# Sigmoid attention and a top-1 mixture of experts in one kernel: attention products in one group per seven steps

## The chip, the core and the metric

The kernel runs on one core of a Trainium2 chip. The metric is device time in microseconds (us) of one execution. Before the change the median of three runs is 801.93 us (801.66 to 802.69).

## What is computed

```
scores = q @ k^T / sqrt(64) - log(448)          # 8 batches x 12 heads, 448 x 64 each
x      = sigmoid(scores) @ v                    # tokens: 3584 rows of 768
logits = x @ w_gate                             # 8 experts
idx    = argmax(logits);  g = softmax(logits)[idx]
out    = g * (relu(x @ w1[idx]) @ w2[idx])      # 768 -> 1024 -> 768, the rows of each expert
```

All is float32 in and out.

## The kernel before

**Attention.** Two heads make a pair (48 pairs, index `g`), and two pairs make a unit (`u`, 24 of them). A unit has seven steps (`ST` = 7, index `s`); a step computes the scores of 64 keys of both pairs against all 448 queries (`scores(s)`, line 573), ScalarE turns them into sigmoids (`squash`, line 558), and `weighted(s)` (line 589) multiplies them with the values. All these products use quarters of TensorE's array (64 x 64), four at a time. Score tiles lie in a ring of four PSUM buffers (`sc`), and the small tiles of the gate lie in the same ring (`small_ps`). Three units make a batch of 448 tokens; a batch has 21 steps (`PB`).

**Loads.** `load_pair` brings k and q of a pair. The first two pairs come by rows and are turned by TensorE (`turn`, line 534), with a copy out of PSUM by VectorE for k and by ScalarE for q (line 537); the others come in blocks of 32 columns and are transposed by VectorE (line 542). `load_values` brings v. Loads are issued on the queues of SyncE (SP), of ScalarE (q of the first pairs) and of GpSimd (k and v of early pairs). `warm_up` issues products on a tile of ones at the start: 34 of them, and 12 more between the two pairs of step 0.

**Gate.** After a batch its logits (`gate_a`, `psg`), the choice (`gate_b`, `pl`), counts (`gate_c`, `pc`), ranks of the tokens within their expert (`gate_d`, `pr`), records scattered to memory (`gate_d2`, line 386, GpSimd indirect DMAs) and the gate's values as rows (`gate_g`, `gate_e`, `pg`, copied by ScalarE at line 415) follow, at steps that the tables `LATE`, `LAST`, `EARLY` and `FIRST_LATE` give: `7: "b"` is stage b at the batch's step 7. I call the products of `pl`, `pc`, `pr` and `pg` the rank products.

**Experts.** Each of seven slots runs all 448 tokens of a batch through one expert, the commonest of that batch (`moe`): 144 products of the first layer (line 213) and 144 of the second (line 236), each 128 x 128 by 448 columns, in parts of high and low bits. Weights are loaded raw, ScalarE casts the high part (line 132) and GpSimd subtracts to get the low part (line 133). What the slots don't cover is sorted into items afterwards, found by prefix sums on VectorE (`tensor_tensor_scan`, line 801), gathered, computed (`large`) and scattered.

**Order.** The whole order is written by hand: each engine gets its instructions in the order in which the program issues them. Up to step 70 (`START`) there is only attention and gate. From there the generator `attention()` yields twice per step and the caller issues 7 products of the experts at each yield (`more`). Attention products come in two groups per unit: at `i == 0` three pieces (24 score and value products of the built program), at `i == 3` five pieces (32). `until(n)` runs the experts' products up to n before the end of the slots.

Of the kernel before, what the change touches and what calls it, by code (L numbers as in the profile page):

```python
# [18 lines left out]
P = 128  # L19
# [5 lines left out]
def tile_sigmoid_attention_top1_moe(  # L25
# [457 lines left out]
    ops = {}  # L483
# [7 lines left out]
    def load_pair(g):  # L491
# [3 lines left out]
        if g < BY_ROWS:  # L495
            for nm, src, eng in (("k", k, nc.sync), ("q", q, nc.scalar)):
                t = apool.tile([P, KC, D], F32, tag=nm + "n", bufs=4, name=f"{nm}n_{g}")
                for h in range(2):
                    eng.dma_start(t[OWN[h]], src[b, 2 * hp + h].rearrange("(p c) d -> p c d", c=KC))
                ops[g, nm + "n"] = t  # L500
            return
# [12 lines left out]
    def load_values(g):  # L514
        if g >= NG or (g, "v") in ops:
            return
        b, hp = divmod(g, NP)
        t = apool.tile([P, KC, D], F32, tag="vn", bufs=4, name=f"vn_{g}")
        for h in range(2):
            eng = nc.gpsimd if 4 <= g < K_POOL else nc.sync  # L520
            eng.dma_start(t[quarter(g, h)], v[b, 2 * hp + h].rearrange("(p c) d -> p c d", c=KC))
        ops[g, "v"] = t

    def turn(g, nm):

        if g >= NG:
            return
        t = apool.tile([P, S], F32, tag=nm + "t", bufs=4, name=f"{nm}t_{g}")
        if g < BY_ROWS:
            rows = ops.pop((g, nm + "n"))  # L530
            ps = ps_moe.tile([P, 512], F32, tag="moe", name=f"turn_{nm}_{g}")
            for c in range(KC):
                for own in OWN:
                    nc.tensor.matmul(
                        ps[own, c * DK : (c + 1) * DK], rows[own, c, :], ident[own, own], start=True, stop=True
                    )
            (nc.vector.tensor_copy if nm == "k" else nc.scalar.copy)(
                t.rearrange("d (p c) -> d c p", c=KC), ps[:, :S].rearrange("d (c p) -> d c p", c=KC)
            )
            ops[g, nm] = t  # L540
            return
        nc.vector.transpose(t, ops.pop((g, nm + "n")).rearrange("p j s -> p (j s)"))
        ops[g, nm] = t

# [19 lines left out]
    def scores(s):  # L564
# [3 lines left out]
        for g, ps in zip(two, pss):  # L568
            if s == 0 and g == 1:
                warm_up(FILL)  # L570
            for h in range(2):
                ks = ops[g, "k"][OWN[h]].rearrange("d (p c) -> d c p", c=KC)[:, c]
                nc.tensor.matmul(ps[quarter(g, h), :S], ks, ops[g, "q"][OWN[h]], start=True, stop=True)  # L573
# [3 lines left out]
    def weighted(s):  # L577
# [22 lines left out]

    WARM, FILL, K_POOL, BY_ROWS = 34, 12, 22, 2
    START = 70
# [8 lines left out]
        1: lambda u: (turn(2 * u + 2, "q"), load_values(2 * u + 2)),  # L611
        3: lambda u: (turn(2 * u + 3, "k"), load_pair(2 * u + 5)),
        4: lambda u: (turn(2 * u + 3, "q"), load_values(2 * u + 3)),
    }

    def attention():
# [4 lines left out]
        warm_up(WARM)  # L621
        load_pair(0)
        load_pair(1)
        for g in range(2):
            turn(g, "k")
            turn(g, "q")
            load_values(g)
# [3 lines left out]
        for g in (2, 3):  # L631
            load_pair(g)
            load_values(g)
        done_av = done_sc = 0
# [35 lines left out]

        LATE = {7: "b", 10: "c", 11: ("l", "c2"), 12: "c3", 14: "d", 16: ("d2", "g"), 17: "e"}
        LAST = {3: "b", 5: "c", 6: ("l", "c2"), 7: "c3", 8: "d", 9: ("d2", "g"), 10: "e"}
        EARLY = {5: "b", 7: ("c", "c2"), 9: ("l", "c3"), 11: "d", 13: ("d2", "g"), 17: "e"}
        FIRST_LATE = {5: "b", 10: "c", 11: ("l", "c2"), 12: "c3", 14: "d", 16: ("d2", "g"), 17: "e"}
        PLACES = {}
# [15 lines left out]
        def stages_late(s):  # L691
            u, i = divmod(s, ST)
            b, r = divmod(s - PB, PB)
            if r == (3 if b < B - 1 else 1) and (b + 1) * PB >= START:
                gate_a(b)
# [3 lines left out]
        for s in range(N_ST + 11):  # L699
# [6 lines left out]
            if s < START:  # L706
                if s % 2 == 0:
# [4 lines left out]
                    score_to(s + 2)  # L712
            elif i == 0:
                stages_late(s)
                score_to(a + 2)
                weigh_to(a)
                score_to(a + 4)
            yield s, MIX[0]
            if s >= START:
                if i > 0:  # L720
                    stages_late(s)
                if i == 3:
                    weigh_to(a + 2)
                    score_to(a + 6)
                    weigh_to(a + 4)
                    score_to(a + 7)
                    weigh_to(a + 5)
            if i in READY and s < N_ST:
# [50 lines left out]
    def cut(n, w=1):  # L779
        return scr[:, n * NI : (n + w) * NI]  # L780
# [19 lines left out]
    for msk, cum in zip((big, few), rank):  # L800
        nc.vector.tensor_tensor_scan(cum, cut(3), msk, 0.0, op0=ALU.mult, op1=ALU.add)
    ends = rest.tile([P, 1], F32, name="ends")
    nc.vector.tensor_scalar(ends, rank[1][:, NI - 1 : NI], 1.0, None, op0=ALU.add)
# [299 lines left out]
```

## Time and profile before

| | |
|---|---|
| runs, median of 3 | 801.93 us |
| profiled execution, its own time | 803.83 us |
| profiled execution, span from first to last instruction | 801.9 us |
| PE (matmul) busy | 789.7 us, 98% |
| DVE, ACT, POOL busy | 355.1, 391.2, 360.3 us |
| DMA queue of SyncE, share of 16 engines | 63.1% |

PE is TensorE's matmul pipe, PEld its weight loads, DVE is VectorE, ACT ScalarE, POOL GpSimd, SP SyncE. A product's busy time runs over its successor's, since products are pipelined: what a product costs is the distance from its start to the next start. Float32 products of the attention stand as two records each in the trace, and as one row in the built order.

### The profile page before, as it was taken

To read this page: it belongs to the slowest core of one execution; us is meant where nothing else is said; L and a number is where in the kernel's file an instruction comes from. 1 tells how busy PE (TensorE), PEld (TensorE's weight loads), DVE (VectorE), ACT (ScalarE), POOL (GpSimd) and SP (SyncE) were. 2 spreads that over 40 slices of the span, in tenths; PEclk is the share of its full clock that TensorE was granted. 3 is DMA by queue.
4 is the path that set the end of the run, shared out by engine and by line. 5 is a ranking of instruction groups with operands and counts; after the bars stand their busy time and mean duration, and the time that the engine had idled before them with its cause. 6 is when DMAs were issued, how large, how long until landed. Compare 5 with 4: busy or idle time off the path is not lost. (4 is left out here: it accounts for less than half of the span.)

```text
span 801.9 us, 15879 instructions
## 1 busy us (share of the span) xinstructions
PE 789.7 (98%) x5726; PEld 613.6 (77%) x5726; DVE 355.1 (44%) x787; ACT 391.2 (49%) x711; POOL 360.3 (45%) x346
## 2 busy tenths in 40 slices
PE   9999999999999999999999999999999999999996
PEld 6655555777787778766777678777788998999996
DVE  2344456462535435362443525355267174334443
ACT  5877777454533554454544545355342342335342
POOL 8658665353223424243242334233553664574350
PEclk9999999999999999999999999999999999999998
DMA  9997998895669937489575874747166445556671
GB/s 178 157 180 129 169 218 183 181 214 110 145 136 200 197 74 166 114 189 183 106 168 99 195 173 113 182 123 182 50 162 169 138 134 158 162 135 176 190 216 38
DMA packets 312372, 124.09 MB, mean 155 GB/s; under 512 B 209502, under 2 KB 309934, under 8 KB 312288
## 3 DMA queue, kind: packets, MB, share of 16 engines
q1 hardware_dynamic: 305920, 110.80, 63.1%
q0 software_dynamic: 6048, 11.76, 6.1%
q8 instruction: 47, 0.77, 0.4%
q10 hardware_dynamic: 320, 0.46, 0.2%
q14 instruction: 37, 0.30, 0.1%
HBM read 100.89 MB, written 22.47 MB: 154 GB/s over the span
## 5 line engine op out<-in xcount | busy, mean ns | idle before, releaser
L558 ACT ACTIVATE at<-sc,bias_s 128x448 f32<-128x448 f32 x336 | 188.2, 640 | 114.2 <-PE sc L573 111.8
L133 POOL TENSOR_TENSOR w1l<-wst,w1h 128x768 fp32r<-128x768 f32 x72 | 132.3, 1846 | 206.5 <-ACT w1h L132 197.4
L133 POOL TENSOR_TENSOR w2l<-wst,w2h 128x512 fp32r<-128x512 f32 x84 | 107.0, 1294 | 155.5 <-ACT w2h L132 155.5
L573 PE MATMUL sc<-qt,kt 64*64 64x448 f32 x1344 | 171.2, 549 | 1.0 <-ACT at L558 0.7
L589 PE MATMUL av<-at,vn 64*64 64x448 f32 x1344 | 167.0, 539 | 0.8 <-ACT at L558 0.7
L573 PEld LDWEIGHTS sc<-qt,kt 64*64 64x64 f32 x1344 | 87.1, 192 | 54.6 <-issue 31.5
L213 PE MATMUL ps<-xh,w1h 128*128 128x448 f32 x336 | 124.2, 370 | 1.8 <-DVE w2s L809 1.3
L213 PE MATMUL ps<-xl,w1h 128*128 128x448 f32 x336 | 123.6, 368 | 0.0
L213 PE MATMUL ps<-xh,w1l 128*128 128x448 f32 x336 | 123.6, 368 | 0.0
L236 PE MATMUL ps<-hh,w2h 128*128 128x448 f32 x336 | 123.3, 367 | 0.0
L236 PE MATMUL ps<-hl,w2h 128*128 128x448 f32 x336 | 123.3, 367 | 0.0
L236 PE MATMUL ps<-hh,w2l 128*128 128x448 f32 x336 | 123.1, 366 | 0.0
L589 PEld LDWEIGHTS av<-at,vn 64*64 64x64 f32 x1344 | 63.4, 133 | 60.1 <-issue 42.2
L132 ACT CAST w2h<-wst 128x512 fp32r<-128x512 f32 x108 | 65.2, 622 | 57.3 <-PE ps L236 43.9
L220 ACT ACTIVATE hh<-ps 128x448 fp32r<-128x448 f32 x56 | 30.6, 547 | 123.3 <-PE ps L213 121.6
L221 DVE SCALAR_TENSOR_TENSOR hl<-ps,hh 128x448 fp32r<-128x448 f32 x56 | 34.8, 621 | 119.8 <-ACT hh L220 113.5
L248 DVE TENSOR_TENSOR ps<-ps,gt 128x448 f32<-128x448 f32 x42 | 26.4, 629 | 136.0 <-PE ps L236 135.9
L213 PEld LDWEIGHTS ps<-xh,w1h 128*128 128x128 f32 x336 | 63.1, 188 | 11.5 <-issue 4.5
L236 PEld LDWEIGHTS ps<-hh,w2h 128*128 128x128 f32 x336 | 65.2, 194 | 7.1 <-issue 3.5
L236 PEld LDWEIGHTS ps<-hl,w2h 128*128 128x128 f32 x336 | 65.2, 194 | 6.6 <-issue 3.7
L236 PEld LDWEIGHTS ps<-hh,w2l 128*128 128x128 f32 x336 | 65.2, 194 | 5.9 <-issue 2.8
L213 PEld LDWEIGHTS ps<-xl,w1h 128*128 128x128 f32 x336 | 63.1, 188 | 8.7 <-issue 3.5
(160 smaller groups left out, 945.3 us busy)
## 6 DMA issues: line engine op xcount, KB each, us to landing
wst<-in_moe_w_dram SPq DMA_DIRECT2D x72, 384.0 KB
wst<-in_moe_w_dram SPq DMA_DIRECT2D x54, 512.0 KB
x_tok<-xt SPq DMA_DIRECT2D x64, 168.0 KB
qn<-in_q_dram SPq DMA_DIRECT2D x184, 56.0 KB
raw<-x_tok SPq DMA_DIRECT2D x28, 336.0 KB
out_dram<-ob SPq DMA_DIRECT2D x84, 112.0 KB
vn<-in_v_dram SPq DMA_DIRECT2D x60, 112.0 KB
kn<-in_k_dram SPq DMA_DIRECT2D x104, 56.0 KB
```

The source lines that it names most:

```text
L132: nc.scalar.copy(hi, st)
L133: eng.tensor_tensor(lo, st, hi.bitcast(F32), op=ALU.subtract)
L213: nc.tensor.matmul(ps[:, :S], a[:, ws], b_, start=(t == 0 and n == 0), stop=(t == KD - 1 and n == 2))
L220: nc.scalar.activation(hh[:, :S], ps[:, :S], AF.Relu)
L221: nc.vector.scalar_tensor_tensor(hl[:, :S], ps[:, :S], 0.0, hh[:, :S].bitcast(F32), op0=ALU.max, op1=ALU.subtract)
L236: nc.tensor.matmul(ps[:, :S], a, b_, start=(j == 0 and n == 0), stop=(j == KF - 1 and n == 2))
L248: nc.vector.tensor_tensor(ps[:, :S], ps[:, :S], gate_rows[b], op=ALU.mult)
L558: nc.scalar.activation(at, ps[:, :S], AF.Sigmoid, bias=bias_s, scale=SCALE)
L573: nc.tensor.matmul(ps[quarter(g, h), :S], ks, ops[g, "q"][OWN[h]], start=True, stop=True)
L589: nc.tensor.matmul(psv[g][OWN[h], :S], ops[g, "v"][rows, c, :], at[rows], start=(c == 0), stop=(c == KC - 1))
```

## The change

From step 70 on the two attention groups of a unit become one, before step 4's second half (`BURST` = 4): seven times the scores of a step and the values of a step two behind, 56 products in a row. Rank products keep their steps roughly (`b` 7 to 8, `d` 14 to 15), and with the groups gone from beside them they now stand between experts' products. The scatters (`d2`) move from step 16 to 19, behind the gate rows (`e`, 17). The other odd pair's turns and loads move one step earlier (`READY` 3, 4 to 2, 3). At the start the first two pairs load k and q in one DMA of 128 rows each instead of two of 64, and all values of even pairs do so everywhere; values come after both pairs; each of the first pairs has PSUM buffers of its own to turn in (`turn_rows`), k is copied as it lies, q is copied half by ScalarE and half by VectorE; 30 warm-up products instead of 34, none in step 0. In the tail 12 experts' products stand behind each prefix sum.

```
         if g < BY_ROWS:
             for nm, src, eng in (("k", k, nc.sync), ("q", q, nc.scalar)):
                 t = apool.tile([P, KC, D], F32, tag=nm + "n", bufs=4, name=f"{nm}n_{g}")
-                for h in range(2):
-                    eng.dma_start(t[OWN[h]], src[b, 2 * hp + h].rearrange("(p c) d -> p c d", c=KC))
+                eng.dma_start(t, src[b, 2 * hp : 2 * hp + 2].rearrange("h (p c) d -> (h p) c d", c=KC))
...
+        eng = nc.gpsimd if 4 <= g < K_POOL else nc.sync
+        if g % 2 == 0:
+            eng.dma_start(t, v[b, 2 * hp : 2 * hp + 2].rearrange("h (p c) d -> (h p) c d", c=KC))
+            ops[g, "v"] = t
+            return
...
+    def turn_rows(g):
+
+        pool, tag = (ps_av, "av") if g else (ps_moe, "moe")
+        pk, pq = (pool.tile([P, 512], F32, tag=tag, name=f"turn_{x}_{g}") for x in "kq")
+        for nm, ps in (("k", pk), ("q", pq)):
...
+        nc.vector.tensor_copy(kt, pk[:, :S])
+        nc.scalar.copy(q_to[:, :4], q_at[:, :4])
+        nc.vector.tensor_copy(q_to[:, 4:], q_at[:, 4:])
...
-    WARM, FILL, K_POOL, BY_ROWS = 34, 12, 22, 2
+    WARM, K_POOL, BY_ROWS = 30, 22, 2
...
-        LATE = {7: "b", 10: "c", 11: ("l", "c2"), 12: "c3", 14: "d", 16: ("d2", "g"), 17: "e"}
+        LATE = {8: "b", 10: "c", 11: ("l", "c2"), 12: "c3", 15: "d", 16: "g", 17: "e", 19: "d2"}
...
-            elif i == 0:
-                stages_late(s)
+            elif s == START:
+                weigh_to(a)
                 score_to(a + 2)
-                weigh_to(a)
-                score_to(a + 4)
             yield s, MIX[0]
             if s >= START:
-                if i > 0:
-                    stages_late(s)
-                if i == 3:
-                    weigh_to(a + 2)
-                    score_to(a + 6)
-                    weigh_to(a + 4)
-                    score_to(a + 7)
-                    weigh_to(a + 5)
+                stages_late(s)
+                if i == BURST:
+                    for n in range(ST):
+                        score_to(a + n + 3)
+                        weigh_to(a + n + 1)
...
     for msk, cum in zip((big, few), rank):
         nc.vector.tensor_tensor_scan(cum, cut(3), msk, 0.0, op0=ALU.mult, op1=ALU.add)
+        more(12)
```

On TensorE, the rank products of batch 4 (`pr_4`) in the order before, between an expert's first layer (`ps1`) and a unit's scores (`sc`):

```order
L213 MATMUL ps1_2_6_4505<-xh_2_0_3770,w1h_2_6_4393 128x448
L213 MATMUL ps1_2_6_4505<-xl_2_0_3771,w1h_2_6_4393 128x448
L360 LDWEIGHTS upper_89
L360 MATMUL pr_4_4508<-lm_4_4432,upper_89 128x32
L361 LDWEIGHTS ones_85
L361 MATMUL pr_4_4508<-lm_4_4432,ones_85 128x32
L573 MATMUL sc_34_0_4525<-qt_34_4242,kt_34_4215 64x448 x2
L573 MATMUL sc_35_0_4526<-qt_35_4434,kt_35_4367 64x448 x2
L573 MATMUL sc_34_1_4535<-qt_34_4242,kt_34_4215 64x448 x2
L573 MATMUL sc_35_1_4536<-qt_35_4434,kt_35_4367 64x448 x2
```

and the same place in the order after:

```order
L213 MATMUL ps1_2_7_4552<-xl_2_0_3774,w1h_2_7_4466 128x448
L213 MATMUL ps1_2_7_4552<-xh_2_0_3773,w1l_2_7_4467 128x448
L213 MATMUL ps1_2_7_4552<-xh_2_1_3789,w1h_2_7_4466 128x448
L213 MATMUL ps1_2_7_4552<-xl_2_1_3790,w1h_2_7_4466 128x448
L360 LDWEIGHTS upper_89
L360 MATMUL pr_4_4558<-lm_4_4328,upper_89 128x32
L361 LDWEIGHTS ones_85
L361 MATMUL pr_4_4558<-lm_4_4328,ones_85 128x32
L213 MATMUL ps1_2_7_4552<-xh_2_1_3789,w1l_2_7_4467 128x448
L213 MATMUL ps1_2_7_4552<-xh_2_2_3817,w1h_2_7_4466 128x448
```

The score tiles that followed `pr` in the ring are gone from behind it: an expert's chain goes on.

On GpSimd, the records of batch 3 (`rec_3`) and their four scatters among the low parts of second-layer weights (`w2l_1_`, numbered 8 to 19), before:

```order
L133 TENSOR_TENSOR w2l_1_11_3564<-wst_1_9_3198,w2h_1_11_3563 128x512
L133 TENSOR_TENSOR w2l_1_12_3570<-wst_1_10_3228,w2h_1_12_3569 128x512
L380 IOTA rec_3_3587 112x4
L386 DMA recs_58<-rec_3_3587,si_3_3446 28672x2 x4
L133 TENSOR_TENSOR w2l_1_13_3726<-wst_1_10_3228,w2h_1_13_3725 128x512
L133 TENSOR_TENSOR w2l_1_14_3738<-wst_1_11_3375,w2h_1_14_3737 128x512
```

and after:

```order
L133 TENSOR_TENSOR w2l_1_13_3714<-wst_1_10_3186,w2h_1_13_3713 128x512
L133 TENSOR_TENSOR w2l_1_14_3726<-wst_1_11_3380,w2h_1_14_3725 128x512
L380 IOTA rec_3_3730 112x4
L386 DMA recs_58<-rec_3_3730,si_3_3497 28672x2 x4
L133 TENSOR_TENSOR w2l_1_15_3751<-wst_1_11_3380,w2h_1_15_3750 128x512
L133 TENSOR_TENSOR w2l_1_16_3763<-wst_1_12_3415,w2h_1_16_3762 128x512
```

The scatters stand two parts later among the weights.

On VectorE, the two prefix sums of the tail (written as scalar-tensor-tensor on `w2s`) and what stands behind them, before; `ps2_5_2_0` is an expert's result that waits to be scaled out of PSUM:

```order
L249 STREAM_TRANSPOSE ob_5_1_7563<-ps2_5_1_1_7612 128x448
L801 SCALAR_TENSOR_TENSOR w2s_7373<-w2s_7373 128x112 x2
L803 TENSOR_SCALAR ends_7684<-w2s_7373 128x1
L804 SCALAR_TENSOR_TENSOR ends_7684<-w2s_7373,ends_7684 128x1
L805 TENSOR_SCALAR w2s_7373<-w2s_7373 128x112
L807 SCALAR_TENSOR_TENSOR w2s_7373<-w2s_7373,slot1_88 128x112 x2
L248 TENSOR_TENSOR ps2_5_2_0_7675<-ps2_5_2_0_7675,gt_5_6788 128x448
L249 STREAM_TRANSPOSE ob_5_2_7674<-ps2_5_2_0_7675 128x448
```

and after:

```order
L249 STREAM_TRANSPOSE ob_5_1_7520<-ps2_5_1_1_7569 128x448
L804 SCALAR_TENSOR_TENSOR w2s_7330<-w2s_7330 128x112 x2
L248 TENSOR_TENSOR ps2_5_2_0_7632<-ps2_5_2_0_7632,gt_5_6710 128x448
L249 STREAM_TRANSPOSE ob_5_2_7631<-ps2_5_2_0_7632 128x448
L807 TENSOR_SCALAR ends_7683<-w2s_7330 128x1
L808 SCALAR_TENSOR_TENSOR ends_7683<-w2s_7330,ends_7683 128x1
L809 TENSOR_SCALAR w2s_7330<-w2s_7330 128x112
L811 SCALAR_TENSOR_TENSOR w2s_7330<-w2s_7330,slot1_88 128x112 x2
```

The expert's result is now taken directly behind the sums, ahead of the four lines that use them.

## Rows read from the trace of the kernel before

**Rows 1.** The page, part 1: busy time, share, instructions of each engine.

```profile
PE 789.7 (98%) x5726; PEld 613.6 (77%) x5726; DVE 355.1 (44%) x787; ACT 391.2 (49%) x711; POOL 360.3 (45%) x346
```

**Rows 2.** Timeline of PE around one attention group: start us, us, line, count.

```profile
210.12 0.37 PE L236 MATMUL ps<-hl,w2h 128*128 128x448 f32 x1
210.41 1.34 PE L263 MATMUL psg<-xf,wg 128*32 128x224 f32 x24
...
213.24 1.68 PE L573 MATMUL sc<-qt,kt 64*64 64x448 f32 x16
214.74 1.68 PE L589 MATMUL av<-at,vn 64*64 64x448 f32 x16
...
217.86 0.48 PE L236 MATMUL ps<-hh,w2l 128*128 128x448 f32 x1
218.18 0.37 PE L236 MATMUL ps<-hh,w2h 128*128 128x448 f32 x1
218.38 0.37 PE L236 MATMUL ps<-hl,w2h 128*128 128x448 f32 x1
```

**Rows 3.** Windows, one per attention group: length, busy us of each engine, clock, DMA.

```profile
211.69:217.86 6.17, 6.17 (x69) 2.82 (x65) 3.13 (x6) 2.79 (x6) 0.01 (x1) 1.00 0.58 148
...
373.83:381.48 7.65, 6.98 (x65) 3.01 (x65) 0.00 (x0) 3.45 (x7) 2.83 (x3) 1.00 0.96 110
391.65:396.38 4.73, 4.73 (x49) 2.19 (x48) 1.97 (x4) 4.13 (x9) 0.00 (x0) 1.00 0.29 69
...
455.81:461.72 5.91, 5.75 (x51) 2.79 (x49) 3.86 (x13) 4.23 (x8) 2.04 (x2) 1.00 1.11 215
553.13:558.20 5.07, 5.07 (x51) 2.83 (x48) 2.68 (x11) 3.95 (x8) 0.81 (x1) 1.00 0.35 103
```

**Rows 4.** Timeline of POOL and ACT in the group that starts at 373.83.

```profile
372.59 0.96 POOL L386 DMA_INDIRECT recs<-rec,si  x1 [1.99 <-DVE gs L405]
...
376.36 0.94 POOL L386 DMA_INDIRECT recs<-rec,si  x1 [0.30 <-issue]
378.56 0.63 ACT L558 ACTIVATE at<-sc,bias_s 128x448 f32<-128x448 f32 x1 [4.09 <-PE sc L573]
```

**Rows 5.** Timeline of PE in the group that starts at 455.81, behind `pr`.

```profile
457.75 0.66 PE L573 MATMUL sc<-qt,kt 64*64 64x448 f32 x2 [0.16 <-DVE rk L369]
```

**Rows 6.** Timeline of PE behind the last attention group: rank products between experts' products.

```profile
598.31 0.38 PE L272 MATMUL pl<-ident,logits 128*112 128x128 f32 x2
598.45 0.46 PE L236 MATMUL ps<-hh,w2l 128*128 128x448 f32 x1
598.74 0.36 PE L236 MATMUL ps<-hh,w2h 128*128 128x448 f32 x1
...
617.81 0.47 PE L213 MATMUL ps<-xh,w1h 128*128 128x448 f32 x1 [0.18 <-DVE hl L221]
```

**Rows 7.** Timeline of DVE and PE around the prefix sums.

```profile
657.42 2.98 DVE L801 TENSOR_TENSOR_SCAN w2s<-w2s 128x112 f32<-128x112 f32 x2
...
662.59 0.62 DVE L248 TENSOR_TENSOR ps<-ps,gt 128x448 f32<-128x448 f32 x1
...
664.04 0.44 PE L213 MATMUL ps<-xh,w1h 128*128 128x448 f32 x1 [1.32 <-DVE w2s L809]
```

**Rows 8.** Timeline of PE, and of DVE at 20.14, at the start.

```profile
1.02 3.81 PE L549 MATMUL ps_warm<-ones 128*128 128x128 bf16 x34 [1.02 <-POOL ones L75]
...
5.87 0.97 PE L534 MATMUL turn_k<-ident,kn 64*64 64x64 f32 x25 [0.63 <-DMA kn<-in_k_dram]
...
10.55 0.84 PE L549 MATMUL ps_warm<-ones 128*128 128x128 bf16 x12
11.32 1.04 PE L573 MATMUL sc<-qt,kt 64*64 64x448 f32 x8
...
20.14 0.65 DVE L542 STREAM_TRANSPOSE qt<-qn 128x448 f32<-128x448 f32 x1 [3.08 <-DMA qn<-in_q_dram]
```

**Rows 9.** The page, part 5: the low parts of the second layer's weights.

```profile
L133 POOL TENSOR_TENSOR w2l<-wst,w2h 128x512 fp32r<-128x512 f32 x84 | 107.0, 1294 | 155.5 <-ACT w2h L132 155.5
```

More of the change, by code (lines that the diff above doesn't have):

```diff
@@ L518, in load_values @@
         t = apool.tile([P, KC, D], F32, tag="vn", bufs=4, name=f"vn_{g}")
+        eng = nc.gpsimd if 4 <= g < K_POOL else nc.sync
[3 more added lines that the diff above has]
+            return
         for h in range(2):
-            eng = nc.gpsimd if 4 <= g < K_POOL else nc.sync
             eng.dma_start(t[quarter(g, h)], v[b, 2 * hp + h].rearrange("(p c) d -> p c d", c=KC))
@@ L528, in turn @@
         t = apool.tile([P, S], F32, tag=nm + "t", bufs=4, name=f"{nm}t_{g}")
-        if g < BY_ROWS:
+        nc.vector.transpose(t, ops.pop((g, nm + "n")).rearrange("p j s -> p (j s)"))
+        ops[g, nm] = t
+    def turn_rows(g):
+        pool, tag = (ps_av, "av") if g else (ps_moe, "moe")
+        pk, pq = (pool.tile([P, 512], F32, tag=tag, name=f"turn_{x}_{g}") for x in "kq")
+        for nm, ps in (("k", pk), ("q", pq)):
             rows = ops.pop((g, nm + "n"))
-            ps = ps_moe.tile([P, 512], F32, tag="moe", name=f"turn_{nm}_{g}")
             for c in range(KC):
@@ L534, in turn @@
                     nc.tensor.matmul(
-                        ps[own, c * DK : (c + 1) * DK], rows[own, c, :], ident[own, own], start=True, stop=True
+                        ps[own, c * DK : (c + 1) * DK], rows[own, c], ident[own, own], start=True, stop=True
                     )
[L537 to L543, printed above, removed]
+        kt, qt = (apool.tile([P, S], F32, tag=f"{x}t", bufs=4, name=f"{x}t_{g}") for x in "kq")
+        q_to = qt.rearrange("d (p c) -> d c p", c=KC)
+        q_at = pq[:, :S].rearrange("d (c p) -> d c p", c=KC)
+        nc.vector.tensor_copy(kt, pk[:, :S])
+        nc.scalar.copy(q_to[:, :4], q_at[:, :4])
+        nc.vector.tensor_copy(q_to[:, 4:], q_at[:, 4:])
+        ops[g, "k"], ops[g, "q"] = kt, qt
     def warm_up(n):
@@ L568, in scores @@
         for g, ps in zip(two, pss):
-            if s == 0 and g == 1:
-                warm_up(FILL)
+            by = "d (c p) -> d c p" if g < BY_ROWS else "d (p c) -> d c p"
             for h in range(2):
-                ks = ops[g, "k"][OWN[h]].rearrange("d (p c) -> d c p", c=KC)[:, c]
+                ks = ops[g, "k"][OWN[h]].rearrange(by, c=KC)[:, c]
                 nc.tensor.matmul(ps[quarter(g, h), :S], ks, ops[g, "q"][OWN[h]], start=True, stop=True)
@@ L611, in tile_sigmoid_attention_top1_moe @@
         1: lambda u: (turn(2 * u + 2, "q"), load_values(2 * u + 2)),
-        3: lambda u: (turn(2 * u + 3, "k"), load_pair(2 * u + 5)),
-        4: lambda u: (turn(2 * u + 3, "q"), load_values(2 * u + 3)),
+        2: lambda u: (turn(2 * u + 3, "k"), load_pair(2 * u + 5)),
+        3: lambda u: (turn(2 * u + 3, "q"), load_values(2 * u + 3)),
     }
+    BURST = 4
     def attention():
@@ L621, in attention @@
         warm_up(WARM)
[L622 to L627, printed above, removed]
+        for load in (load_pair, load_values):
+            load(0)
+            load(1)
+        turn_rows(0)
+        turn_rows(1)
         nc.gpsimd.memset(wg, 0.0)
@@ L630, in attention @@
         setup()
-        for g in (2, 3):
-            load_pair(g)
-            load_values(g)
+        for load in (load_pair, load_values):
+            load(2)
+            load(3)
         done_av = done_sc = 0
@@ L669, in stage @@
                 gate_e(b - 1, g["gs"])
-        LATE = {7: "b", 10: "c", 11: ("l", "c2"), 12: "c3", 14: "d", 16: ("d2", "g"), 17: "e"}
+        LATE = {8: "b", 10: "c", 11: ("l", "c2"), 12: "c3", 15: "d", 16: "g", 17: "e", 19: "d2"}
         LAST = {3: "b", 5: "c", 6: ("l", "c2"), 7: "c3", 8: "d", 9: ("d2", "g"), 10: "e"}
         EARLY = {5: "b", 7: ("c", "c2"), 9: ("l", "c3"), 11: "d", 13: ("d2", "g"), 17: "e"}
-        FIRST_LATE = {5: "b", 10: "c", 11: ("l", "c2"), 12: "c3", 14: "d", 16: ("d2", "g"), 17: "e"}
+        FIRST_LATE = {5: "b", 10: "c", 11: ("l", "c2"), 12: "c3", 15: "d", 16: "g", 17: "e", 19: "d2"}
         PLACES = {}
@@ L693, in stages_late @@
             b, r = divmod(s - PB, PB)
-            if r == (3 if b < B - 1 else 1) and (b + 1) * PB >= START:
+            if r == (BURST if b < B - 1 else 1) and (b + 1) * PB >= START:
                 gate_a(b)
```

## The prediction

> **What bounds the kernel now.** I read the page's part 1 first: PE is busy 98% of the span [rows 1]. So only what PE itself does, or a wait inside it, can move the end, and the list of waits names almost none. But a PE that counts as busy need not be at its pace, so I went to the timeline of PE from step 70 on (136.49 to 665.43) and took distances between starts. An expert's product starts 0.20 us after the one ahead of it (218.18 to 218.38), and 16 records of attention take 1.50 us (213.24 to 214.74), 0.0938 each [rows 2]. Whatever exceeds these two paces is loss that the busy share hides. Two kinds stand out: the edges of each attention group, and groups that are longer than others with the same work [rows 3]. Then I looked at the start and at the tail, where PE does stand still.
>
> **Edges of a group.** A clean group of 32 products of the built order (64 records) takes 6.17 us, its records at pace 64 x 0.0938 = 6.00: 0.17 inside. A clean group of 24 takes 4.73 against 4.50: 0.23 inside [rows 3]. Behind it the first expert's product takes 0.32 to the next start instead of 0.20: 0.12. Where an expert's product directly precedes something of another array shape, it takes 0.29 (210.12 to 210.41): 0.09 [rows 2]. From step 70 the built order has 29 groups before and 15 after. 14 fewer x (0.20 + 0.12) = 4.5 us gained. Of the groups, or the logits ahead of one, 10 followed an expert's product directly and 15 do now: 5 x 0.09 = 0.45 lost. Net 4.0 gained; ends 3.4 (every edge at the cheaper 0.17, entries dearer by half) and 4.9. Experts' and attention products themselves are as many as before.
>
> **Rank products alone.** 19 more of them stand between experts' products. The tail of before shows such a place: `pl` takes 0.14 from its start to the next, and the expert's product behind it 0.29 instead of 0.20, an edge of 0.09 [rows 6]. Beside a group they also took their length, and the group's edge came on top, so I count the move at nothing, between 1.7 lost (19 x 0.09) and 1.7 gained. The Trainium skill, in "TensorEngine Tiling (Array Packing)", Key Properties, says that changing the tiling mode drains TensorE, while another tile in the same mode does not. By that, `pl`, which uses the array whole like the expert's product, should have no edge; the 0.09 speaks against it here, and I go by the row.
>
> **Waits inside groups.** Read like rows 3, the 28 full groups exceed their clean lengths by 6.5 us together; twelve carry it, the plain ones behind `pr` 0.34 each (5.07 against 4.73), the largest 1.18 (5.91) and 1.48 (7.65 against 6.17) [rows 3]. Two causes show. First, `pr` lies in the ring of score tiles: a score product waits until VectorE has read the ranks (`rk`) [rows 5]. With `pr` between experts' products, 56 of them pass before the next score tile wants that buffer after `pg`, some 11 us. Second, the group behind `pg`: ScalarE starts its first squash at 378.56, after 4.09 us idle and 1.26 after the last of four scatters ended (376.36 + 0.94) [rows 4]. That is a coincidence in time, not a wait that I can name; the program makes the squash wait only for PE. The scatters leave the group now, and `pg` gets 14 products (2.8 us) before the group to be copied out. I take 5.3 of the 6.5, with 2.5 (only `pr` cured) and 6.5 as ends. Inside the longer group ScalarE has two squashes per step, by rows 3 at most 4.13 us busy in a group of 4.73, a step takes PE 16 x 0.0938 = 1.50, and score tiles run two steps ahead; so I add no wait.
>
> **Tail.** VectorE runs both prefix sums (2.98 us) and four more lines before it can empty the expert's result at 662.59, and PE stands 1.32 us at 664.04 [rows 7]. After, the result stands directly behind the sums, and its chain ends 18 products (3.6 us) after the sums begin: they are over by then. 1.3 gained; ends 0 (the wait shows at the next result, behind the four lines) and 1.5. The 24 products are taken from a later stretch of 140 that only has to cover transposes; nothing else moves.
>
> **Start.** PE waits for the second half of k (0.63 us idle before 5.87), later bridges q of the second pair with 12 warm-up products, and runs attention steadily from 11.32 [rows 8]. One DMA per tile brings the second half with the first; PSUM buffers of their own and q copied by two engines take away the rest: from 1.4 (0.63 + 0.77) to 1.9 us earlier. But the second unit needs q of pair 3, whose transpose waited 3.08 us for its DMA at 20.14 [rows 8]. If transfers set that, only what moves behind q counts: v of pair 2, 229 KB, at 148 to 219 GB/s [rows 3] 1.0 to 1.5 us (an estimate). So 1.1; ends 0 and 1.9.
>
> **New waits.** VectorE's chains behind the rank products now run while experts need it for `hl`; in the tail of before one such wait shows, 0.18 us idle on PE [rows 6]. Five batches x 0.2 = 1.0 lost; ends 0 and 2.5. On GpSimd four scatters hold 372.59 to 377.30, 4.71 us [rows 4], and a low part takes 1.29 [rows 9]: 6.0, while a part is issued 24 products (4.9 us) ahead of its use. Scatters of batches 2 and 3 begin 23 and 24 products before the first such part is used plus what was queued earlier, so the excess is a few tenths: 0.4 for both, ends 0 and 2.2.
>
> **Sum.** 4.0 + 5.3 + 1.3 + 1.1 - 1.0 - 0.4 = 10.3 us. The profiled execution took 803.83 for a span of 801.9, 1.9 outside it and 1.9 above the median; its own time becomes 793.5, and the median 801.93 - 10.3 = 791.6.
>
> **Rivals.**
> - *The squash comes late for another reason than the scatters* (chance 0.12). For it: DMA is at 0.96 and 1.11 in the long groups and 0.29 to 0.58 in the clean ones [rows 3], and the loads stay. Against: 553.13 is long at 0.35, so DMA alone does not set it. Then 2.5 instead of 5.3 comes back, and one long group per unit keeps its waits: 801.93 - 7.5 = 794.4, and with the hidden start 795.5.
> - *TensorE's clock rises later* (0.08). The 34 warm-ups took 3.81 us, 112 ns each, the 12 later ones 0.84, 70 each [rows 8]: the engine ran at the lower of its levels (1.2 GHz) first and at the upper (2.4 GHz) by 10.55, after a pause that ended at 5.87. 30 warm-ups and none later could leave the turns and first scores, some 4.5 us between 5.87 and 11.32, at the lower level; at up to twice the time that costs 2 to 4.5 us: 794 to 796. The Trainium skill's "TensorE: Matmul & The Clock Gate", Part 1, holds that throttled is the default and activity releases it, which speaks against dropping warm-ups; no row here shows it fall once risen.
> - *By the tiling rule* (0.05). If rank products between experts' products have no edge, 1.7 more comes back: 789.9.
> - *Low parts late behind the scatters; slower* (0.04). Place: the second layer in batches 2 to 6, where no attention group covers the scatters any more. If every batch loses the whole hold, 5 x 4.71 = 23.6, the time is 801.93 - 10.7 + 23.6 = 814.8. It turns slower than before at 2.2 us per batch. Against: parts are issued at least 24 products ahead, and only two or three fall behind the scatters.
> - *Terms cancel* (0.02): the low ends of waits, start and tail with the high ends of new waits leave about nothing, 801.
>
> **Chances and range.** The forecast has 0.69. All cases but the last two end below by more than 0.2% (1.6 us, about what a measurement of this kernel tells from no change): faster 0.94, within 0.03, slower 0.03. The low end takes every upper end: 4.9 + 6.5 + 1.5 + 1.9 = 14.8, less 0.4: 787.5. The high end takes in the first two rivals: 797.
>
> **What would show it.** From step 70 to the last attention group: 15 groups, of 10.5 + 0.2 us each; no score product behind `pr` that waits for `rk`; squashes about 1 us behind their scores throughout; no wait of PE over 1 us behind the prefix sums; steady attention from about 9.5 instead of 11.32. Wrong it would be if groups run over 11.5 us, if PE waits for `w2l` parts in the second layer, or if the turns of the first pairs run at 60 ns instead of 30 per record.

## The result and the profile after

The change makes the kernel slower: 809.37 us, median of 8 runs (806.41 to 812.69), against 802.37 (801.28 to 804.62); ratio 1.0085, 95% interval 1.006 to 1.011. The forecast was 791.6, with 787.5 to 797 as its range. The profiled execution spans 809.1 us, 7.2 more than before.

PE is busy 97% now, and the list of PE's waits, which held nothing over 1.3 us in total before, has four large entries (engine, line, what is waited for; total us, times, longest):

```profile
PE ps L213 <- DVE hl L221: 4.8, 2, 2.4
PE ps L236 <- POOL w2l L133: 4.3, 3, 1.9
PE ps L236 <- DVE ob L249: 3.9, 4, 1.3
PE sc L581 <- DVE logits L267: 1.4, 1, 1.4
```

The first three lie where no attention stands; the fourth, for the logits, lies at the start of an attention group. Windows of the kernel after (length, busy us of each engine, clock, DMA share, GB/s): three of the stretches of 98 experts' products between a group and the gate's logits, a clean group, a group that waits, 28 products within the last batch's gate, and 114 products of the tail.

```profile
187.04:210.87 23.83, 21.97 (x102) 20.11 (x99) 15.76 (x25) 9.77 (x19) 12.88 (x12) 0.93 0.53 118
286.19:310.80 24.61, 20.95 (x102) 18.77 (x98) 17.85 (x28) 10.34 (x19) 14.32 (x13) 1.00 0.52 118
485.96:507.81 21.85, 20.60 (x103) 18.78 (x99) 15.00 (x27) 10.26 (x19) 15.65 (x14) 1.00 0.55 120
443.61:454.35 10.74, 10.74 (x114) 4.91 (x113) 2.23 (x6) 7.53 (x14) 1.41 (x1) 1.00 0.94 230
409.98:423.12 13.14, 11.77 (x117) 6.02 (x113) 0.93 (x2) 8.70 (x15) 1.36 (x1) 1.00 0.82 177
615.57:624.00 8.43, 6.02 (x31) 5.22 (x31) 7.71 (x26) 2.53 (x4) 2.91 (x4) 1.00 1.06 232
673.88:701.29 27.41, 25.05 (x115) 22.70 (x115) 9.62 (x10) 8.72 (x15) 18.16 (x14) 0.94 0.66 187
```

The group is what was hoped for: 112 records at 0.0938 make 10.5, and 10.74 is 0.24 more [rows 3]; ten of the thirteen full groups take 10.74 or 10.75. But 98 products need 20.14 us where nothing waits (the same stretch in a kernel below), and here three take 23.83, 24.61 and 21.85. All excesses in the middle add up to 19.0 us: 3.7, 4.5, 1.4 and 1.7 in four stretches of 98, 1.6 in the gate and first scores behind the second, 2.4 in one group, 1.0 and 2.7 around the last batch's gate. In the tail 114 products take 27.41 for 23.2: 4.2 more.

The first stretch shows what happens. Rows of GpSimd, VectorE and PE in order of time (start us, us, engine, line; idle before and its releaser in brackets):

```profile
192.20 1.01 POOL L386 DMA_INDIRECT recs<-rec,si  x1 [0.28 <-POOL rec L380]
...
196.03 0.94 POOL L386 DMA_INDIRECT recs<-rec,si  x1 [0.30 <-issue]
196.10 0.37 PE L236 MATMUL ps<-hl,w2h 128*128 128x448 f32 x1
196.97 3.76 POOL L133 TENSOR_TENSOR w2l<-wst,w2h 128x512 fp32r<-128x512 f32 x3
198.33 0.60 PE L236 MATMUL ps<-hh,w2l 128*128 128x448 f32 x1 [1.86 <-POOL w2l L133]
198.47 2.75 DVE L444 TENSOR_TENSOR xl<-whole,xh 128x448 fp32r<-128x448 f32 x1 [0.63 <-ACT xh L443]
198.73 0.57 PE L236 MATMUL ps<-hh,w2h 128*128 128x448 f32 x1
```

A window of the products behind that wait, its columns as above (the clock is the third number from the end):

```profile
198.80:201.80 3.00, 3.00 (x10) 2.66 (x9) 2.98 (x2) 0.00 (x0) 1.93 (x2) 0.50 0.31 77
```

Four scatters hold GpSimd from 192.20 to 196.97, four to five microseconds as in [rows 4]; three low parts are owed behind them, and PE waits 1.86 us for the first. While GpSimd works them off, VectorE's subtraction for the next slot's tokens takes 2.75 us instead of 0.63 and ends when GpSimd's last part does (196.97 + 3.76 = 200.73) plus 0.49. And in the window TensorE's granted clock is 0.50, its lower level, behind the wait: ten products at 0.37 us instead of 0.20 cost another 1.7 us. In the second stretch PE waits 1.80 us for a low part at 297.41, the subtraction takes 3.21 us, and VectorE empties an expert's result late enough that PE waits 1.25 us for `ob` at 310.40.

The granted clock falls to 0.50 in two more places: behind that wait of 1.25 us, where the gate's products and the first scores lose the 1.6 us listed above, and in the tail behind a wait of 2.35 us at 695.97, where nine products lose 1.5 us:

```profile
311.20:314.50 3.30, 3.30 (x32) 1.27 (x28) 1.23 (x3) 0.00 (x0) 1.67 (x1) 0.50 1.06 207
696.90:700.20 3.30, 3.30 (x10) 2.95 (x9) 0.00 (x0) 0.00 (x0) 2.94 (x3) 0.50 0.75 208
```

At the start there is no second run of warm-ups, and the turns run without a stop. Attention begins at 7.81 and runs steadily from 9.25, behind a wait of 0.49 us for q; before it ran steadily from 11.32 [rows 8].

```profile
1.02 3.23 PE L558 MATMUL ps_warm<-ones 128*128 128x128 bf16 x30 [1.02 <-POOL ones L75]
4.53 1.03 PE L543 MATMUL turn_k<-ident,kn 64*64 64x64 f32 x28 [0.27 <-DMA kn<-in_k_dram]
5.36 1.01 PE L543 MATMUL turn_q<-ident,qn 64*64 64x64 f32 x28
...
7.81 0.57 PE L581 MATMUL sc<-qt,kt 64*64 64x448 f32 x2
...
9.25 1.34 PE L581 MATMUL sc<-qt,kt 64*64 64x448 f32 x10 [0.49 <-DVE qt L551]
```

### The profile page after: what moved, and what is told of

It is laid out like the page before. It is cut to its first block, busy times and chain, and to the rows that moved or that the text cites. A ratio compares the mean times of both kernels' runs of the same rounds, so it can differ in the third digit from the quotient of the medians.

```text
span 809.1 us, 15766 instructions
## 1 busy us (share of the span) xinstructions
PE 785.1 (97%) x5710; PEld 608.0 (75%) x5710; DVE 362.4 (45%) x789; ACT 395.0 (49%) x711; POOL 356.4 (44%) x337
## 5 line engine op out<-in xcount | busy, mean ns | idle before, releaser
L567 ACT ACTIVATE at<-sc,bias_s 128x448 f32<-128x448 f32 x336 | 192.9, 634 | 95.9 <-PE sc L581 94.7
L581 PE MATMUL sc<-qt,kt 64*64 64x448 f32 x1344 | 175.9, 548 | 1.9 <-DVE logits L267 1.4
L597 PE MATMUL av<-at,vn 64*64 64x448 f32 x1344 | 174.4, 537 | 1.1 <-ACT at L567 1.1
L581 PEld LDWEIGHTS sc<-qt,kt 64*64 64x64 f32 x1344 | 83.2, 189 | 58.7 <-issue 41.2
L457 DVE STREAM_TRANSPOSE xt<-av 128x448 f32<-128x448 f32 x48 | 28.6, 630 | 175.0 <-ACT xf L604 171.6
L213 PEld LDWEIGHTS ps<-xh,w1l 128*128 128x128 f32 x336 | 63.6, 189 | 5.4
```

The lines of the kernel that those rows point to most:

```text
L213: nc.tensor.matmul(ps[:, :S], a[:, ws], b_, start=(t == 0 and n == 0), stop=(t == KD - 1 and n == 2))
L457: nc.vector.transpose(xts[b][:, :, t, :], pv[:, :S].rearrange("p (j s) -> p j s", s=32))
L567: nc.scalar.activation(at, ps[:, :S], AF.Sigmoid, bias=bias_s, scale=SCALE)
L597: nc.tensor.matmul(psv[g][OWN[h], :S], ops[g, "v"][rows, c, :], at[rows], start=(c == 0), stop=(c == KC - 1))
```

## Experiments: the place of the scatters

Ratios are to the kernel before, run beside each on the same chip.

**Scatters back at step 16 of the changed kernel.**

```diff
-        LATE = {..., 15: "d", 16: "g", 17: "e", 19: "d2"}
+        LATE = {..., 15: "d", 16: ("d2", "g"), 17: "e"}
```

> The changed kernel with the scatters back beside the gate's values (step 16 of a batch, ahead of the gate rows) and nothing else. Theory 1: the scatters at step 19 are behind both kinds of waits, GpSimd's low parts that come late and VectorE's work that is held while GpSimd works off the parts it owes. Then the 98 products that stretched to 23.83 us (187.04) and 24.61 us (286.19) fall to their 20.1, and the slow gate and scores behind the second go: 3.7 + 4.5 + 1.6 = 9.8 us gained, about 799.6. Theory 2: the tokens of the next slot (transpose, cast, subtraction, six times in one stretch without attention) overload VectorE by themselves. Then only the direct waits for w2l at 198.33 and 297.41 with the lower clock behind them go, about 5.7 us: 803.7, and waits of PE for ob stay. If the scatters in front of a group make its squashes late as they did before the change, about 1 us per batch comes on top of either.

Measured: 798.18 us, ratio 0.9945 (0.992 to 0.9971), some 11 us faster than the changed kernel. Theory 1 holds for most of it: the stretch at 188.73 takes 20.14, all groups but two take 10.74 to 10.75, and no token subtraction takes over 0.91. Since the scatters now stand ahead of 14 experts' products instead of beside attention, no squash is late. Of theory 2 a part is left: three stretches still take 22.04, 21.81 and 21.76, with waits for `ob`.

**The kernel before with scatters at step 19.** The same one line, in the other kernel.

> The kernel before with its scatters moved from step 16 to 19 and nothing else, its attention in two groups per unit as it was. Theory of the prediction (scatters ahead of a group make its squashes late): the groups that took 7.16 (275.26), 7.65 (373.83), 6.43 (472.26) and 6.25 (178.96) fall to 6.17, 2.8 us gained, about 799.6, if the next group, 28 products behind, covers the low parts. Rival 1: the squashes are late for another reason, these groups stay long, and the time stays at 802 to 803. Rival 2: the low parts come late behind the scatters here too, and the time grows to 804 to 808; then the position of the scatters is bad by itself, not by the longer groups.

Measured: 801.64, ratio 0.9974 (0.9964 to 0.9984): 2.1 us faster. The four groups named take 6.17 or 6.18 now, 2.8 us less together; two others took longer in this execution (5.47 and 6.62 instead of 4.82 and 6.37). Against [rows 4], in the group that started at 373.83 and starts at 371.85 here, ScalarE's first squash comes 1.0 us behind the first score, not 3.2 (378.56 behind the score of before in the first fence; the second is the new kernel):

```profile
375.39 1.68 PE L573 MATMUL sc<-qt,kt 64*64 64x448 f32 x16
```

```profile
373.40 1.68 PE L573 MATMUL sc<-qt,kt 64*64 64x448 f32 x16
...
374.43 2.21 ACT L558 ACTIVATE at<-sc,bias_s 128x448 f32<-128x448 f32 x4 [1.94 <-PE sc L573]
```

So the squash is late with the scatters in front of the group and not without them, as the forecast took it; through what, no row tells. And step 19 is not bad by itself: with two groups per unit no low part came late. It is bad only where 98 products follow without attention. Each half of the change is harmless or good alone; together they cost.

## Experiments: VectorE in the long stretch

**Tokens spread wider.**

```diff
-                    if d == 1 and b + 1 < NS and (8 * t + j) % 3 == 0:
-                        split_tokens(b + 1, (8 * t + j) // 3)
+                    if d and b + 1 < NS and (16 * d + 8 * t + j - 16) % 5 == 0 and 16 * d + 8 * t + j < 46:
+                        split_tokens(b + 1, (16 * d + 8 * t + j - 16) // 5)
```

> The changed kernel with the six tokens of the next slot split every 15 products over two thirds of the second layer, instead of every 9 products in its middle third. Theory 2 (these tokens overload VectorE where no attention stands between): the waits of PE for ob at 310.40, 407.08, 504.96 and 599.62 and for logits at 413.89 go, 1.5 + 0.8 + 2.4 + 1.4 + 0.9 = 7.0 us gained, about 802.4; the waits for w2l at 198.33 and 297.41 stay. Theory 1 (the scatters alone): within 1.5 us of the changed kernel, 808 to 811, with ob still awaited.

Measured: 808.80, ratio 1.0053 (1.0034 to 1.0072). Theory 2 fails as a cause by itself: with the scatters where they were, one subtraction was held longer still, again to GpSimd's end (398.59 + 5.03 = 403.62) plus 0.49, and another took 5.40 us (from 596.20). PE still waits 2.9 us for `ob`, against 3.9.

```profile
398.59 5.03 POOL L133 TENSOR_TENSOR w2l<-wst,w2h 128x512 fp32r<-128x512 f32 x4
399.43 4.68 DVE L444 TENSOR_TENSOR xl<-whole,xh 128x448 fp32r<-128x448 f32 x1 [0.63 <-ACT xh L443]
```

**The subtraction one tile later, so that VectorE does not stand while ScalarE casts;** with scatters at 16 (`pipe`) and at 19 (`pipe_19`).

```diff
             nc.scalar.copy(xh, whole)
-            nc.vector.tensor_sub(xl, whole, xh.bitcast(F32))
+            late_low()                          # the subtraction of the tile before
+            waiting.append((xl, whole, xh))
```

> The changed kernel with the scatters at step 16 (as in scatter_16) and the subtraction of each token tile issued one tile later, so VectorE does not stand while ScalarE casts. In scatter_16 three stretches of 98 products still take 22.04, 21.81 and 21.76 us instead of 20.14, because PE waits for ob (1.25, 0.72, 1.24) and w2l (0.39); there VectorE works off six tiles of 1.80 us each, 0.63 of it idle for ScalarE. Theory 2b: those idle pieces (6 x 0.63 = 3.8 us per stretch) are what makes VectorE late. Then the stretches fall to 20.1 to 20.3, 5 us gained on scatter_16's 798.2: 793, ratio to the kernel before 0.988. Rival: VectorE is late by the sheer number of its instructions there (turns of k and q, results, tiles), or the parts behind ScalarE set the pace: 797 to 798, waits for ob remain.

> The changed kernel, scatters at step 19 as it has them, with the subtraction of each token tile one tile later alone. Theory 1 (the scatters' place sets most of the loss): the waits for w2l at 198.33 and 297.41 stay (1.86 and 1.80 us with the clock's fall behind them), VectorE is still held by the parts that GpSimd owes, and the time falls by 3 to 5 us at most, 804 to 806. Theory 2 (VectorE's idle pieces set it): it falls by as much as from scatter_16 to pipe and by the VectorE waits behind the scatters too, to 799 or lower.

Measured: `pipe` 796.38, ratio 0.9900 (0.9885 to 0.9916); `pipe_19` 808.83, ratio 1.0073 (1.0057 to 1.0089). What was left in scatter_16 was VectorE's idle pieces (0.63 in each of six tiles): all four stretches of `pipe` take 20.13 to 20.14. Rows of scatter_16, where the result stands behind tiles that wait for ScalarE and PE waits, then a window of that stretch in scatter_16 and in `pipe`:

```profile
302.49 0.60 DVE L441 STREAM_TRANSPOSE whole<-raw 128x448 f32<-128x448 f32 x1
303.73 0.62 DVE L444 TENSOR_TENSOR xl<-whole,xh 128x448 fp32r<-128x448 f32 x1 [0.63 <-ACT xh L443]
304.27 0.62 DVE L248 TENSOR_TENSOR ps<-ps,gt 128x448 f32<-128x448 f32 x1
304.93 0.65 DVE L249 STREAM_TRANSPOSE ob<-ps 128x448 f32<-128x448 f32 x1
305.64 0.47 PE L236 MATMUL ps<-hh,w2h 128*128 128x448 f32 x1 [1.25 <-DVE ob L249]
```

```profile
284.00:306.04 22.04, 20.69 (x102) 18.86 (x98) 15.09 (x27) 10.35 (x19) 10.45 (x8) 1.00 0.62 144
```

```profile
282.79:302.93 20.14, 20.14 (x103) 18.94 (x99) 14.85 (x27) 10.42 (x19) 13.13 (x9) 1.00 0.57 123
```

That is less gained than the 5 us expected, because the tail took some back: from the third gate's logits to `pli` (line 826 of the kernel after, where I let the middle end), `pipe` takes 537.9 us in the profile and scatter_16 541.2, but 114 products of the tail take 27.51 us in `pipe` and 23.21 in scatter_16.

The same edit with scatters at 19 gains next to nothing, where Theory 1 had expected 804 to 806: it still waits 1.87, 1.82 and 1.03 us for `w2l`. The scatters come first, VectorE's idle pieces second.

## Experiments: start, tail, and what the long group is worth

**The start alone** (with single loads and earlier turns, all else as before).

> The kernel before with the new start, the single loads of values and the earlier turns of odd pairs alone; groups, tables and tail as before the change. The first expert's product came at 131.61 after the change and at 136.49 before. If the start and the loads make those 4.9 us, and nothing in the middle depends on them: 802.4 - 4.9 = 797.5, first expert's product at 131.6. If 3 us of them come from the steps of the gate's stages in the first batches instead (moved by the same change), it stands at 134.5 and the time is 800.4. If VectorE or the loads collide in the middle because of the earlier turns, the middle (first expert's product to the last gate's pli, 528.94 before) grows.

Measured: 802.24, ratio 0.9973 (0.9961 to 0.9985), 2.2 us by the ratio; neither of the two sums came. The first gate's logits come at 45.76 instead of 47.63, the third's at 122.24 instead of 123.50, the first expert's product at 135.24. The 4.9 us that I had read from the first expert's product were partly a matter of order: from the third gate's logits to it the kernel before takes 136.49 - 123.50 = 12.99, and the kernel after 10.68, because it moves attention from there into its groups.

**The tail without products behind the sums.**

```diff
         nc.vector.tensor_tensor_scan(cum, cut(3), msk, 0.0, op0=ALU.mult, op1=ALU.add)
-        more(12)
```

> The changed kernel without the 12 products behind each prefix sum, so its tail is issued as before the change. Theory: the wait of 2.35 us at 695.97 and the lower clock behind it (27.41 us for 114 products that need 23.3) come because VectorE's copies of gathered rows now meet GpSimd's low parts of weights; with the old order they don't meet and 4.0 us come back, less 1.3 for the old wait behind the sums: 2.7 gained, about 806.7. Rival: these copies meet GpSimd by the accident of where the tail begins, and the added products have nothing to do with it: 1.3 lost, 810.7.

Measured: 807.74, ratio 1.0042 (1.0027 to 1.0056). The number suits the theory: in this run 114 products take 23.21 us, and a wait of 1.34 us behind the sums is back. Yet the added products are not the cause: scatter_16 keeps them and its 114 products take 23.21 too, while `pipe` keeps them and takes 27.51. So in this the rival holds, though its 810.7 did not come. What decides whether the copies of gathered rows meet GpSimd's parts, no run shows. In the kernel after they did:

```profile
690.03 5.34 DVE L868 COPY w2s<-xg 128x768 f32<-128x768 f32 x2 [2.48 <-DMA xg<-x_tok,rec]
690.72 3.76 POOL L133 TENSOR_TENSOR w2l<-wst,w2h 128x512 fp32r<-128x512 f32 x3
...
695.97 0.47 PE L213 MATMUL ps<-xh,w1h 128*128 128x448 f32 x1 [2.35 <-DVE hl L221]
```

**Two memsets later in the tail** (`pipe_tail`: `memset(xg)`, `memset(xgs)` behind `until(330)`, not ahead of it).

> As pipe, and the two memsets of the gathered rows (1.34 and 0.70 us on VectorE) stand behind the experts' products that run up to 330 before the end, not ahead of the result hl. In scatter_16 PE waits 2.40 us for hl at 612.71; ahead of that hl VectorE spends 1.84 us on a product that takes 0.18 elsewhere, and 1.34 on the memset. Theory: the wait falls by the memset, to 1.1, and the time by 1.3 against pipe, about 791.7. Rival: GpSimd's parts hold VectorE by as much at the next place, and nothing is gained: as pipe, 793.

Measured: 795.76, ratio 0.9903 (0.9888 to 0.9918), not to be told from `pipe`. The wait for `hl` fell from 2.39 to 0.87, but this run waits 1.4 us for logits in two groups, and 2.95 for the copies above.

**Two copies to ScalarE** (`final`), and **the same with two groups per unit** (`two_groups`).

```diff
-        nc.vector.tensor_copy(logits, psg[:, :GH])
+        nc.scalar.copy(logits, psg[:, :GH])
...
-            sort_rows(xp[t], xg[:, t])
+            sort_rows(xp[t], xg[:, t], nc.scalar.copy)
```

> pipe_tail, and two of VectorE's copies done by ScalarE: the logits out of PSUM behind the gate's products, and the two rows tiles of the first sorted item in the tail. In pipe_tail PE waits 2.95 us for hl at 682.54 (114 products take 26.43 us, 23.2 elsewhere) and two groups take 12.25 and 12.63 us, 10.74 elsewhere, behind a wait for logits. Theory: both waits are VectorE's, one because its copy is held while GpSimd works off low parts, one because the copy stands behind a result that waits for its store; on ScalarE neither happens: 3.2 + 3.4 = 6.6 us gained, about 789 to 790, ratio 0.983. Rival: the waits move to what stands behind on VectorE or to squashes behind the copy on ScalarE, and the time stays at 793 to 796.

> As final, but attention in two groups per unit with the gate's steps as before the change (scatters at 19, where they did not disturb these groups). What the long group itself is worth, with everything else cured. The prediction's terms: 4.0 us at the edges of groups and 1.8 of the waits inside groups that lie behind the rank products (the scatters' part is cured here too), so 5 to 6 us slower than final, about 795. Rival: edges cost less than taken, and it stands within 2 us of final.

Measured: `final` 790.49, ratio 0.9855 (0.9836 to 0.9874), the fastest here and faster than both kernels; `two_groups` 796.51, ratio 0.9914 (0.9901 to 0.9927). In `final` all groups take 10.74 to 10.75, all stretches of 98 take 20.13 to 20.14, and PE's list of waits has left of the four entries:

```profile
PE ps L213 <- DVE hl L221: 2.0, 2, 1.1
```

The difference of the two, 6.0 us by the medians and 6.9 by the profiled spans, is what the regrouping is worth with the gate's steps that go with it. The expectation's terms were 4.0 + 1.8, but that the sum fits is partly luck. From the third gate's logits to `pli`, where both issue the same products, `two_groups` takes 541.7 us and `final` 533.8. By distances between starts, attention takes 6.9 us less, rank products 2.3 less, and experts' products 1.3 more (in `final` PE waits 0.88 us for `hl` at 604.54). Of the 6.9, 3.2 are waits behind `pr`, not 1.8: the groups there take 5.07, 5.08, 5.76, 5.90 and 5.07 in `two_groups` instead of 4.73. In the tail `final` gives 1.4 us back, with a wait of 1.10 us for `hl` at 676.55.

## Experiments: what holds VectorE

GpSimd's four subtractions beside VectorE's instructions, behind the last store of scatter_16.

```diff
+        for beside in (0, 4):
+            for kind in ("turn", "sub", "sub_psum", "copy", "scalar"):
+                nc.vector.memset(a0, 1.0)
+                for _ in range(beside):
+                    nc.gpsimd.tensor_sub(low, a0, a1)
+                for _ in range(5):
+                    held(kind)
```

> scatter_16 with some 40 us of extra instructions behind its last store: on VectorE five at a time of a transpose, a subtraction of two tiles in SBUF, one with one tile in PSUM, a copy and a multiplication by a constant (all 128x448), first alone, then while GpSimd works off four subtractions like its low parts. Theory: VectorE's instruction with two tiles in SBUF is held until GpSimd is done with all it has in hand (not one instruction, but the run of four, some 4.5 us), and so is the copy; transposes and the one with a tile in PSUM are not. Rival 1: each waits for one GpSimd instruction at most, some 1.2 us. Rival 2: nothing is held, and what took 2.7 to 3.2 us instead of 0.63 waited for something that the trace does not name.

Five of each on VectorE (128x448), a row alone and a row beside GpSimd: a transpose, a subtraction in SBUF, one with a tile in PSUM, a copy. The fifth kind, a multiplication by a constant, went like the copy: 0.39 us alone and 1.20 beside GpSimd.

```profile
799.47 3.30 DVE L1089 STREAM_TRANSPOSE w2s<-w2s 128x448 f32<-128x448 f32 x5
803.17 3.20 DVE L1091 TENSOR_TENSOR w2s<-w2s 128x448 f32<-128x448 f32 x5
806.76 3.19 DVE L1093 TENSOR_TENSOR w2s<-probe_ps,w2s 128x448 f32<-128x448 f32 x5
810.35 2.04 DVE L1095 COPY w2s<-w2s 128x448 f32<-128x448 f32 x5
...
815.21 3.31 DVE L1089 STREAM_TRANSPOSE w2s<-w2s 128x448 f32<-128x448 f32 x5
820.68 6.42 DVE L1091 TENSOR_TENSOR w2s<-w2s 128x448 f32<-128x448 f32 x5
827.50 3.19 DVE L1093 TENSOR_TENSOR w2s<-probe_ps,w2s 128x448 f32<-128x448 f32 x5
832.91 5.26 DVE L1095 COPY w2s<-w2s 128x448 f32<-128x448 f32 x5
```

So GpSimd does hold VectorE, by what the instruction reads: two tiles in SBUF, or a copy or a multiplication by a constant within SBUF, are held; a transpose, or a tile in PSUM, is not. The Trainium skill says the same in "SBUF — State Buffer", Who interferes with whom: an instruction with two SBUF inputs contends with a GpSimd instruction that reads SBUF, and the loser blocks for the whole instruction. The longest single one here was 1.43 us, which suits one instruction (GpSimd's took up to 1.39).

> scatter_16 with extra instructions behind its last store, now in the forms of the kernel: GpSimd works off four low parts (128x512, reduced float32 out), and VectorE, after one, two or three transposes (0.63 each, so that it comes at different places of GpSimd's first or second part), issues one subtraction as for the tokens (128x448) or one copy of 768 columns. In the second probe the subtraction took 0.63 us beside GpSimd, but came within 0.15 us of the end of GpSimd's first instruction. Theory A (held until GpSimd's run is over): one transposes ahead gives 4.4 us, two 3.8, three 3.1 for the subtraction; the copy likewise. Theory B (held to the end of the part under way): 0.6 to 1.9 us in each, and what held VectorE longer in the changed kernel was something else that stands between GpSimd's parts there.

Measured: 1.34, 0.62 and 1.27 us for the subtraction, 1.16 and 1.21 for the copy: Theory B. Three more probes show no longer hold, each with one subtraction: GpSimd in other forms (at most 0.63), GpSimd writing four tiles so that its instructions need not wait for each other (0.62 to 1.34), and with a cast by ScalarE, TensorE's products or loads beside it (0.62 to 1.29). They test it weakly, though: in the first of the three, and wherever a cast stood ahead, the subtraction began within 0.17 us of the end of a GpSimd instruction. And in the kernel after and in tokens_wide single subtractions were held through two to four parts (2.70, 2.75, 3.21, 4.68 and 5.40 us), each to 0.48 to 0.50 behind the last; that is longer than one instruction, and the measurement decides. Not every hold in a kernel is so long: in `pipe` a subtraction at 580.45 took 2.01 us and ended while GpSimd was at its next part. What makes a hold outlast one part is not settled.

## Why the prediction was wrong

**New waits: the step that failed.** I wrote that scatters of batches 2 and 3 begin 23 and 24 products before the first low part used, plus what was queued, "so the excess is a few tenths: 0.4 for both, ends 0 and 2.2", and took 1.0 for VectorE. Measured: 1.86 and 1.80 us of waiting for `w2l` alone, and with VectorE's waits and the clock 19.0 us in the middle and 4.2 in the tail. Four things were wrong. The lead was too long: by my figures 6.0 us against 23 and 24 products (4.7 and 4.9) leaves 1.3 and 1.1, and only the unpriced "what was queued earlier" made it a few tenths. In the trace it is the other way round: in both places the scatters came directly behind a low part on GpSimd and only 20 products (4.1 us) start between the first scatter and the wait. I priced the scatters by GpSimd's own queue, and not by who else is held while GpSimd catches up; yet the trace of before has such rows, a subtraction of one column that lasts as long as a low part:

```profile
607.78 1.85 POOL L133 TENSOR_TENSOR w1l<-wst,w1h 128x768 fp32r<-128x768 f32 x1 [7.09 <-ACT w1h L132]
607.87 1.78 DVE L337 TENSOR_TENSOR free<-free,keep 128x1 f32<-128x1 f32 x1
```

I looked at `hl` on VectorE, not at the tiles of the next slot, which fall into the same 98 products and had an attention group of 4.7 to 4.9 us among them before. And I priced a wait at its length, where TensorE fell to half the clock in three places (1.7, 1.6 and 1.5 us).

The experiments, in the order in which the edits were added, divide the loss. From the third gate's logits to `pli` the profiled executions take 552.4 us in the changed kernel, 541.2 with scatters at 16, 537.9 in `pipe` and 533.8 in `final`. So 11.3 of the 19.0 us hang on the place of the scatters, 3.3 on VectorE's idle pieces and 4.0 on the memsets and copies of the last two edits.

**The slower rival had half of the mechanism.** "Low parts late behind the scatters; slower", given 0.04, named GpSimd and the second layer without attention; it put the place in batches 2 to 6 and turned slower at 2.2 us per batch. It had the waits for low parts (4.3 us in all), not what VectorE and the clock added. Its chance was too small, and its argument against (only two or three parts fall behind the scatters) was true and not enough: two or three parts in a row were what held VectorE.

**Edges.** Forecast 4.0. Not measured alone; what the account leaves for them, with the rank products in it, is 4.6: from the third gate to `pli`, less 24 products (4.9), the profile gives 547.5 against 541.9, so 5.6 more = 19.0 of new waits - 8.8 of old ones that are gone (6.5 in groups, 2.3 elsewhere) - 4.6. The exit still takes 0.31 to the next start and the entry 0.30. `two_groups` against `final` bears out the size of edges and waits together, not of each.

**Rank products.** Counted at nothing, which the rows bear out. They cost an edge of 0.09 to 0.10 each, as in [rows 6], `pl` too, so the rival by which they have none failed. In return they take less themselves: beside a group `pl`, `pc`, `pr` and `pg` took 0.31, 0.12, 0.15 and 0.48 us to the next start, now 0.13, 0.04, 0.07 and 0.32. In the kernel after:

```profile
600.75 0.38 PE L272 MATMUL pl<-ident,logits 128*112 128x128 f32 x2
600.88 0.46 PE L236 MATMUL ps<-hh,w2l 128*128 128x448 f32 x1
601.18 0.36 PE L236 MATMUL ps<-hh,w2h 128*128 128x448 f32 x1
```

**Waits inside groups.** Forecast 5.3 of 6.5; all 6.5 went, in both places named: no score waits for `rk`, and scatter_19 shows the scatters' share by itself (2.1 us by the runs). For `pr` alone I had 2.5; the five groups behind it exceeded 4.73 by 3.2 together. In their place one group waited for logits (2.4, counted above).

**Tail.** The wait behind the sums went (1.3, as forecast): the result is emptied at 664.96, between the two sums' end and the four lines. What I did not see is that the copies of gathered rows can meet GpSimd's parts there (27.41 us for 114 products instead of 23.21).

**Start.** Forecast 1.1, ends 0 and 1.9; alone it measures 2.2 by the ratio (1.2 to 3.1 by its interval), and in the profile 1.9 at the first gate's logits, 1.3 at the third's and 1.1 in the span (801.9 to 800.8). So 1.1 lies near the low end of what is measured, and whether transfers set a part of it is open. (I read 219 GB/s where [rows 3] go to 215, which changes nothing.) The rival by which the clock rises later did not show in the profiled execution of the kernel after, where the first turns run from 4.53 to 5.36, 28 records of 30 ns. It did in other executions of the same start. In `pipe` the first 28 take 1.52 us, 54 ns each, and attention begins at 8.90 instead of 7.81:

```profile
4.60 1.76 PE L553 MATMUL turn_k<-ident,kn 64*64 64x64 f32 x28 [0.20 <-DMA kn<-in_k_dram]
6.12 1.32 PE L553 MATMUL turn_q<-ident,qn 64*64 64x64 f32 x28
```

So its mechanism is there, at about 1 us and not at the 2 to 4.5 that it was priced at.

## What to carry to other kernels

Attention between the experts' products was not only a cost at its edges; it was the time in which GpSimd and VectorE caught up. Before grouping such work, sum up for the longest stretch left without it what the other engines must do there, in order and with their waits for each other, and keep bursts on GpSimd (scatters, and what is owed behind them) out of that stretch. With scatters moved, one subtraction and two memsets delayed and two copies on another engine, the same grouping gained 6.0 us instead of losing.

## What was not expected of the hardware

- An instruction of VectorE with two SBUF tiles, held by GpSimd through a run of up to four parts (5.40 us for 0.63) in a kernel, and through one only (at most 1.43) in the probes.
- ScalarE's first sigmoid 3.2 us behind its score while scatters are issued by GpSimd, 1.0 us without, though the trace shows no wait that ties them.
- TensorE at clock 0.50 for ten products behind an idle 1.86 us (198.33), at 1.00 behind 1.80 us (297.41), and at 0.50 again behind 1.25 us (310.40), all in the same execution.
